# An FFT, a max-of-three layer and a SoLU layer on one core: the weight and first-batch preparation is rebuilt

## The chip, the core and the metric

The kernel runs on one core of a Trainium2 chip. The core has TensorE (PE: matmuls into PSUM; its weight loads are listed apart as PEld), VectorE (DVE), ScalarE (ACT), GpSimd (POOL) and SyncE (SP), whose queue issues every transfer here. Each engine works through its instructions in the order in which they were written. The metric is the device time of one execution in microseconds (us); less is better.

## The reference

```python
def reference(x, moe_w1, moe_w2, moe_w3, moe_w_out, moe2_w_in, moe2_w_out, moe2_g_ln):
    X = np.fft.fft(np.fft.fft(x, axis=1), axis=2).real     # x: 8 x 3072 x 256, f32
    x = X.reshape(8 * 3072, 256)
    h = np.maximum(np.maximum(x @ w1, x @ w2), x @ w3)     # 256 -> 768
    x = h @ w_out                                          # 768 -> 256
    h = x @ w_in                                           # 256 -> 1024
    e = np.exp(h - h.max(-1)); solu = h * e / (e.sum(-1) + 1e-9)
    ln = (solu - mean) / np.sqrt(var + 1e-6) * g_ln
    return ln @ w_out2                                     # 1024 -> 256
```

The weights come as float64, the inputs as float32.

## The kernel before

Each f32 operand is split into two f16 halves (high and low), and a product is three f16 matmuls. The FFT over the sequence is a matmul with a table (`alpha`, over 48 rows), a transposing transfer (`z`) and a second table (`beta`). The FFT over the 256 columns and the sum over real and imaginary parts are folded into the weights ahead of the main work: w1 - w3 and w2 - w3 are multiplied with a cosine and sine table (`wc`), w3 is multiplied with that table (`t3`) and then with w_out (`m3`).

The main work runs over 48 sub-blocks s of 512 rows, six for each of the 8 batches. One sub-block takes two `beta` parts, 14 groups of six `l` matmuls of layer 1 (operations `l1`; two groups for each of six column blocks j, and two with the folded w3), six `m` groups of layer 1's output, four `h` tiles of layer 2's input (12 matmuls each) and four `o` tiles of its output (24 each). Between them ACT, DVE and POOL evacuate (two PSUM buffers hold the `l` groups), take the maximum (`rl`, DVE), split into halves (`rh` on ACT, `rlo` on POOL), and do the exponentials.

Ahead of that stands the **preparation**. `from_f64` turns a weight into f32: a load into a `raw` buffer (`ld`, two buffers), a first pass on ACT (`ga`: magnitude of the high word) and four passes on DVE (`gd`: a maximum, a shift with a mask, and two that merge the high and low words). Then come the subtractions (`sub`, on POOL), `wc`, `t3`, `m3`, the search for each weight's scale (`am`, `dg`, a `spread` matmul, `pow`), and the split into halves. Batch 0 of x goes through `xla` (load), `xgh` (a sum, on DVE), `xfly` (two sums and differences, on POOL), `xsq` (ACT, for the scale), `xsc` (the scale), `xhi`/`xlo` (halves; the low half of chunks 1 and 3 on POOL through `X_POOL`), and `alpha` with its halves `ah` (ACT) and `alo` (DVE).

The order on each engine is written by a planner. `Schedule.run` holds a table of operations with an engine, a planned duration, dependencies, buffers to take and give, and a due value (`vt`, plus an entry of the table `BIAS`); at each step it emits, on the engine that can start first, the operation that ranks first by start and due value. What it emits is a fixed order; on the chip only semaphores delay an instruction. The buffers of the preparation lie in a pool (`prep`) that the second layer's buffers overlay: the operation `open` waits for all operations that were entered with `pop`, and `mh` (the halves for the first `h`) waits for `open`. In this kernel the preparation of w_out2 (operations `f`, `wfg`, `wfm`, `wfs`, `wfn`, `wfh`, `wfl`) is one of them.

Of the kernel before, what the change touches and what calls it, by code (L numbers as in the profile page):

```python
# [1317 lines left out]
```

## Time and profile before

| | us |
|---|---|
| median of 3 runs (2029.46 to 2032.61) | 2031.4 |
| the profiled execution | 2030.42 |
| its span, first to last instruction | 2028.3 |
| PE busy in the span | 1954.3 (96%) |
| DVE / ACT / POOL busy | 1722.3 / 1481.2 / 1343.4 |

About 2 us of the profiled execution lie around the span. Matmuls are pipelined, so that PE's busy time says that it has work in it, not that it is at its peak; PEclk is the TensorE clock that was granted (1.0 is 2.4 GHz, 0.5 is 1.2 GHz).

### The profile page before, as it was taken

To read this page: it belongs to the slowest core of one execution; us is meant where nothing else is said; L and a number is where in the kernel's file an instruction comes from. 1 tells how busy PE (TensorE), PEld (TensorE's weight loads), DVE (VectorE), ACT (ScalarE), POOL (GpSimd) and SP (SyncE) were. 2 spreads that over 40 slices of the span, in tenths; PEclk is the share of its full clock that TensorE was granted. 3 is DMA by queue.
4 is the path that set the end of the run, shared out by engine and by line. 5 is a ranking of instruction groups with operands and counts; after the bars stand their busy time and mean duration, and the time that the engine had idled before them with its cause. 6 is when DMAs were issued, how large, how long until landed. Compare 5 with 4: busy or idle time off the path is not lost.

```text
span 2028.3 us, 40637 instructions
## 1 busy us (share of the span) xinstructions
PE 1954.3 (96%) x14892; PEld 1344.3 (66%) x14892; DVE 1722.3 (85%) x3894; ACT 1481.2 (73%) x2933; POOL 1343.4 (66%) x1408
## 2 busy tenths in 40 slices
PE   3679999999999999999999999999999999999998
PEld 2446666666667666766667666676667666666666
DVE  6878989888898888888888988889888888888884
ACT  3768877877678767786678776787667766766766
POOL 4199986976559756795567856575656565655654
PEclk9789999999999999999999999999999999999999
DMA  7523653543435434444434443333344243333236
GB/s 214 140 64 81 131 115 76 118 95 74 79 69 121 94 69 80 92 113 77 73 72 97 95 84 74 74 63 75 83 74 79 64 84 74 69 74 74 53 69 125
DMA packets 472698, 178.79 MB, mean 88 GB/s; under 512 B 453577, under 2 KB 453802, under 8 KB 469290
## 3 DMA queue, kind: packets, MB, share of 16 engines
q1 hardware_dynamic: 472498, 176.20, 41.7%
q8 instruction: 116, 1.90, 0.4%
q14 instruction: 84, 0.69, 0.1%
HBM read 37.75 MB, written 25.17 MB: 31 GB/s over the span
## 4 chain that ended last, share of the span: by engine, by line
PE 84%; POOL 5%; DVE 5%; ACT 3%; issue 2%; DMA 2%; SPq 0%; POOLq 0%; DVEq 0%; ACTq 0%
PE h L784 22%; PE omm L859 21%; PE l L654 20%; PE m L720 16%; PE beta L549 2%; PE alpha L490 1%; POOL uh L472 1%; POOL xs L410 1%; POOL uv L452 1%; POOL vh L845 1%; POOL rhl L710 1%; DVE v L814 1%; DVE l L675 1%; DMA raw<-in_w_dram 1%; DVE hst L793 1%
## 5 line engine op out<-in xcount | busy, mean ns | idle before, releaser
L710 POOL TENSOR_TENSOR rhl<-sv,rhl 128x512 f16<-128x512 f32 x288 | 333.4, 1160 | 344.2 <-ACT rhl L705 317.5
L859 PE MATMUL omm<-wf,vt 128*128 128x256 f16 x4608 | 533.3, 273 | 1.8 <-ACT ob L866 1.0
L784 PE MATMUL h<-win,mo 128*128 128x512 f16 x2280 | 523.2, 379 | 2.1 <-DVE v L814 2.1
L859 PEld LDWEIGHTS <-vt 128*128 128x128 f16 x4608 | 450.2, 98 | 78.8 <-issue 1.7
L845 POOL TENSOR_TENSOR vh<-v,vh 128x1024 f16<-128x1024 f32 x188 | 400.6, 2131 | 110.8 <-ACT vh L841 107.5
L654 PE MATMUL l<-pq,wl 128*128 128x256 f16 (+2 forms) x3456 | 447.6, 273 | 11.8 <-DVE sv L701 8.1
L675 DVE SCALAR_TENSOR_TENSOR l<-ny,wn,l 128x256 f32<-128x256 f32 (+1 forms) x672 | 318.0, 482 | 148.0 <-ACT bs L367 126.6
L720 PE MATMUL m<-rhl,wo 128*128 128x512 f16 x1728 | 415.2, 380 | 0.0
L654 PEld LDWEIGHTS <-wl 128*128 128x128 f16 x3456 | 332.1, 97 | 111.1 <-issue 10.5
L784 PEld LDWEIGHTS <-mo 128*128 128x128 f16 x2304 | 223.9, 98 | 239.0 <-DVE v L814 3.4
L367 ACT ACTIVATE bs<-l 128x256 f32<-128x256 f32 x560 | 207.4, 380 | 209.2 <-PE l L654 163.9
L819 ACT ACTIVATE jk<-v,hst 128x1024 f16<-128x1024 f32 x192 | 220.1, 1146 | 87.0 <-DVE v L814 86.9
L814 DVE SCALAR_TENSOR_TENSOR v<-h,hst,e 128x1024 f32<-128x1024 f32 x190 | 243.3, 1281 | 29.1 <-ACT e L808 17.0
L720 PEld LDWEIGHTS <-wo 128*128 128x128 f16 x1728 | 163.3, 98 | 151.9 <-issue 1.6
L793 DVE TENSOR_REDUCE hst<-h 128x1 f32<-128x1024 f32 x190 | 231.4, 1218 | 31.6 <-PE h L784 30.3
L808 ACT ACTIVATE e<-h,hst,xb 128x1024 f32<-128x1024 f32 x190 | 228.9, 1205 | 6.4
L841 ACT CAST vh<-v 128x1024 f16<-128x1024 f32 x192 | 200.0, 1042 | 6.0 <-DMA vt<-vh 4.3
L701 DVE SCALAR_TENSOR_TENSOR sv<-l,sv 128x512 f32<-128x512 f32 x288 | 198.2, 688 | 5.7
L705 ACT CAST rhl<-sv 128x512 f16<-128x512 f32 x288 | 176.1, 613 | 35.7 <-DVE sv L701 18.7
L735 POOL TENSOR_TENSOR mo<-s,mw 128x512 f16<-128x512 f32 x96 | 121.6, 1276 | 16.7 <-ACT mw L367 12.2
L832 POOL TENSOR_SCALAR hst<-hst,sc 128x1 f32<-128x1 f32 x192 | 68.1, 354 | 68.7 <-ACT jk L819 56.2
L695 DVE SCALAR_TENSOR_TENSOR sv<-l,bs 128x256 f32<-128x256 f32 x240 | 100.9, 420 | 12.2 <-POOL rhl L710 3.7
(156 smaller groups left out, 2316.2 us busy)
## 6 DMA issues: line engine op xcount, KB each, us to landing
xs<-in_x_dram SPq DMA_DIRECT2D x32, 768.0 KB, 6.3
out_dram<-ob SPq DMA_DIRECT2D x96, 256.0 KB, 2.0
raw<-in_w_dram SPq DMA_DIRECT2D x6, 768.0 KB, 5.0
raw<-in_w_out_dram SPq DMA_DIRECT2D x14, 256.0 KB, 3.4
vt<-vh SPq DMA_TRANSPOSE x192, 4.2
raw<-in_w_in_dram SPq DMA_DIRECT2D x4, 512.0 KB
cb<-in_c_beta_dram SPq DMA_DIRECT2D x1, 1553.0 KB
z<-x SPq DMA_TRANSPOSE x48, 3.3
```

Of the source, the lines that this page charges most:

```text
L367: act.activation(dst, src, AF.Copy, scale=scale)
L654: mm(o, w_[w], hl[:, a, e, c0:c0 + n_], start=(n == 0), stop=(n == 2))
L675: dve.scalar_tensor_tensor(p[:, 0:WA], pq[s][1][:, 0:WA], w, p[:, 0:WA], ALU.mult, ALU.add)
L710: pool.tensor_tensor(t[:, 1], svs.pop((s, j, 0)), t[:, 0], ALU.subtract)
L720: mm(m[:, h], wo[:, w, j, hs], t[:, a], start=(j == 0 and n == 0), stop=(j == NJF - 1 and n == 2))
L784: mm(hp[:, f], m[:, a, d, ts_], win[:, w, d, fs], start=(n == 0), stop=(n == 5))
L793: dve.tensor_reduce(st[:, 0], y["h"], op=ALU.max, axis=AX.XY, negate=True)
L808: act.activation(y["e"], y["h"], AF.Exp, bias=st[:, 11], scale=xbt[s // NSB][:, 12:13], accum_out=st[:, 3])
L814: dve.scalar_tensor_tensor(y["v"], y["h"], st[:, 2], y["e"], ALU.mult, ALU.mult, accum_out=st[:, 4])
L819: act.activation(new(hpool[0], "jk", [128, 2, 512], F16), y["v"], AF.Square, bias=st[:, 4], scale=-float(FF2), accum_out=st[:, 6])
L845: engine.tensor_tensor(y["vh"][:, 1], y["v"].rearrange("p a b -> p (a b)"), y["vh"][:, 0], ALU.subtract)
L859: mm(y["o"][:, 0:D], vt[:, a * 8 + c], wf[:, w, c], start=(n == 0), stop=(n == 23))
```

## The change

The preparation and the start of batch 0 are rewritten:

- **Conversion.** ACT multiplies the high word by 2^-112, which leaves the exponent ready; DVE needs three passes in place of four (the maximum goes, the mask goes with the shift).
- **Buffers.** `raw` has three buffers in place of two, and the two loads of w1 use the memory of `x1`, five in all. w_out2 is loaded into buffers of x (`xs`) and converted into buffers of `uv`, as two pieces of 1024 columns in place of four of 512; its operations, `gl` and `mean` are out of the `prep` pool, so `open` doesn't wait for them. `st` has 8 buffers in place of 9.
- **GpSimd.** `sub` and, for batch 0, `xfly` and all four `xlo` run on DVE. For later batches they stay on POOL.
- **Queue.** `cw` (the cosine table) is loaded first; `cal` (the alpha table) later, and in two pieces of 96 rows and 1. `gl` is loaded in one contiguous piece. Batch 1's loads wait for `open`.
- **Zeros.** Where the planner sees PE idle ahead of an operation, up to the first `h`, `keep_warm` enters matmuls of 512 columns on a tile of zeros (`zz`), for 75% of the planned gap at 216 ns each.
- **The planner's numbers.** Many planned durations are altered and every entry of `BIAS` (some 250) is replaced, so that all orders change.

```diff
-EXP_MIN = float(np.array(0x38000000, np.int32).view(np.float32))
+EXP_SHIFT = 2.0**-112
...
-                vh=2, vt=3, ob=2, xb=4, dg=1, raw=2, st=9)
-X_POOL = (0, 1, 0, 1)
+                vh=2, vt=3, ob=2, xb=4, dg=1, raw=3, st=8)
...
-BIAS = {("xla", 0): -477.352, ("xgh", 0): 585.07, ("xfly", 0): 58.101, ("xsq", 0): 186.462, ("xhi", 0): 986.332,
...
+BIAS = {("xla", 0): -534.137, ("xgh", 0): 286.232, ("xfly", 0): -6.751, ("xsq", 0): 385.004, ("xhi", 0): 285.602,
...
-PORT = {"gd", "wlo", "w3l", "vl", "xgh", "xlo"}
+PORT = {"gd", "sub", "wlo", "w3l", "vl", "xgh", "xfly", "xlo"}
...
+            if o.eng == "PE" and self.idle:
+                self.idle(k, start - clock["PE"])
...
+    def x_buffer():
+        return new(fp, "xs", [128, GC * 2 * D], F32)
...
+    def uv_buffer():
+        return new(fp, "uv", [128, 4 * D], F32)
...
-        t = new(fp, "xs", [97, GC, 2, D], F32)
+        t = x_buffer()[0:97].rearrange("p (g w d) -> p g w d", g=GC, w=2)
...
-    def x_fly(b, c):
+    def x_fly(b, c, engine):
...
-        u = new(fp, "uv", [97, 2, GC, 128], F32)[0:n]
+        u = uv_buffer()[0:n].rearrange("p (h g d) -> p h g d", h=2, g=GC)
         for h, o in enumerate((ALU.add, ALU.subtract)):
-            pool.tensor_tensor(u[:, h], t[:, :, 0:128], t[:, :, 128:256], o)
+            engine.tensor_tensor(u[:, h], t[:, :, 0:128], t[:, :, 128:256], o)
...
-        op(("xla", *k), "SP", 3500, x_load, k, v - 0.5, deps=[("xla", b, c - 1)] if c else [("xla", b - 1, NCH - 1)] * (b > 0) + [("gd", "f", 3)] * (b == 1),
...
-        op(("xfly", *k), "Pool", 2450, x_fly, k, v - 0.2, deps=[("xgh", *k)], take=["uv"], give=["xs"])
+        op(("xla", *k), "SP", 3500 if b else 2600, x_load, k, v - 0.5, deps=[("xla", b, c - 1)] if c else [("xla", b - 1, NCH - 1)] * (b > 0) + [("open",), ("gd", "f", 1)] * (b == 1),
...
+        op(("xfly", *k), *(("Pool", 2450) if b else ("DVE", 1200)), x_fly, (*k, pool if b else dve), v - 0.2, deps=[("xgh", *k)], take=["uv"], give=["xs"])
...
-        normed = 1 if b else X_POOL[c]
+        normed = b > 0
...
-                op(("al", *kh), "PE", 520, alpha_mm, kh, v + 0.04 * h, deps=[("xlo", b, c)] + [("al", b, 0, 0)] * (not first) + [("al", b, c, 0)] * h,
+                op(("al", *kh), "PE", 520, alpha_mm, kh, v + 0.04 * h, deps=[("xlo", b, c), ("cal",)] + [("al", b, 0, 0)] * (not first) + [("al", b, c, 0)] * h,
...
-        sp.dma_start(cal, c_alpha)
+        sp.dma_start(cal[0:96], c_alpha[0:96])
+        sp.dma_start(cal[96:97], c_alpha[96:97])
...
-    ones = tp.tile([128, 128], F32, name="ones")
+    zz = wp.tile([128, 512], F16, name="zz")
+    pool.memset(zz, 0.0)
+    ones = wp.tile([128, 128], F32, name="ones")
...
-    const_load()
+    op(("cal",), "SP", 900, const_load, (), -0.85, lag=2000)
...
+    def f64_home(key, home):
+        if home == "raw":
+            return new(tp, "raw", [128, FF, 2], I32)
+        if home == "xs":
+            return x_buffer().bitcast(I32).rearrange("p (m w) -> p m w", w=2)
+        if home not in homes:
+            homes[home] = new(fp, "x1", [128, NSB, 2, 4, 128], F16).rearrange("p s h q x -> p (s h q x)").bitcast(I32)
+        return homes[home][:, key[-1] * 2 * FF:(key[-1] + 1) * 2 * FF].rearrange("p (m w) -> p m w", w=2)
...
-        def magnitude():
-            act.activation(dst(), raws[key].bitcast(F32)[:, 0:n, 1], AF.Abs)
-
-        slow, fast = 80 + 1.145 * n, 110 + 0.585 * n
-        return magnitude, [
-            (fast, lambda: dve.tensor_scalar(dst(), dst(), EXP_MIN, None, ALU.max)),
-            (fast, lambda: dve.tensor_scalar(bits(), bits(), 3, 0x3FFFFFFF, ALU.logical_shift_left, ALU.bitwise_and)),
-            (slow, lambda: dve.scalar_tensor_tensor(bits(), word(1), -0x40000000, bits(), ALU.bitwise_and,
+        def exponents():
+            act.activation(dst(), raws[key].bitcast(F32)[:, 0:n, 1], AF.Copy, scale=EXP_SHIFT)
+
+        slow, fast = 15 + 1.135 * n, 30 + 0.6 * n
+        return exponents, [
+            (fast, lambda: dve.tensor_scalar(bits(), bits(), 3, None, ALU.logical_shift_left)),
+            (slow, lambda: dve.scalar_tensor_tensor(bits(), word(1), -0x80000000, bits(), ALU.bitwise_and,
                                                     ALU.bitwise_or)),
             (slow, lambda: dve.scalar_tensor_tensor(bits(), word(0), 29, bits(), ALU.logical_shift_right,
                                                     ALU.bitwise_or)),
         ]
...
-        pop(("ld", *key), "SP", 4.4 * n, f64_load, (key, srcs, n), v - 0.2, deps=after, take=["raw", *take], lag=2000)
...
+        put(("ld", *key), "SP", 3.4 * n, f64_load, (key, srcs, n, home), v - 0.2, deps=after, take=[home] * first + [*take], lag=1900)
...
-        pool.tensor_tensor(wrs[i, a], wrs[i, a], wrs[0, a], ALU.subtract)
+        dve.tensor_tensor(wrs[i, a], wrs[i, a], wrs[0, a], ALU.subtract)
...
-            from_f64((i, a), [w[a * 128:(a + 1) * 128]], w_first(i, a), FF, -0.9 + 0.1 * i + 0.03 * a, take=["st"])
+            from_f64((i, a), [w[a * 128:(a + 1) * 128]], w_first(i, a), FF, -0.9 + 0.1 * i + 0.03 * a, take=["st"],
+                 **(dict(home="x1", first=a == 0, after=[("ld", 1, 0)] * a, done=[("gd", 1, 0)] * a, give=[("x1", ("ld", 1, 0))] * a) if i == 1 else {}))
...
-            pop(("sub", i, a), "Pool", 1760, w_sub, (i, a), v, deps=[("gd", i, a), ("gd", 0, a)])
+            pop(("sub", i, a), "DVE", 890, w_sub, (i, a), v, deps=[("gd", i, a), ("gd", 0, a)])
...
-            pop(("wc", i, a), "PE", 4000, w_dft, (i, a), v, take=["mh"[a]],
+            pop(("wc", i, a), "PE", 2600, w_dft, (i, a), v, take=["mh"[a]],
...
-        pop(("m3", e), "PE", 5100, w3_mm, (e,), -0.5,
+        pop(("m3", e), "PE", 2620, w3_mm, (e,), -0.5,
...
-    gl = tp.tile([128, 8], F32, name="gl")
-    pop(("gl",), "SP", 600, lambda: sp.dma_start(gl, g_ln.rearrange("(c p) -> p c", p=128), allow_slow_non_contiguous=True), (), 0.0,
-        lag=2500)
+    gl = wp.tile([128, 8], F32, name="gl")
+    op(("gl",), "SP", 400, lambda: sp.dma_start(gl, g_ln), (), 0.0, lag=2000)
...
-        for c in (2 * u, 2 * u + 1):
+        for c in range(4 * u, 4 * u + 4):
...
-    for u in range(4):
...
+    for u in range(2):
...
-        from_f64(("f", u), [w_out2[c * 128:(c + 1) * 128] for c in (2 * u, 2 * u + 1)], staged(w2r, u // 2, slice(u % 2 * 512, (u % 2 + 1) * 512)),
-                 512, v, take=[] if u % 2 else ["st"], after=[("ld", "f", u - 1)] if u else staged_first)
-        pop(("wfg", u), "ACT", 800, wf_gain, (u,), v, deps=[("gd", "f", u), ("gl",)])
-    pop(("wfm",), "PE", 5300, wf_mean, (), 0.5, deps=[("wfg", u) for u in range(4)], take=["misc"])
-    pop(("wfe",), "ACT", 270, wf_mean_ev, (), 0.5, deps=[("wfm",)], give=["misc"])
+        from_f64(("f", u), [w_out2[c * 128:(c + 1) * 128] for c in range(4 * u, 4 * u + 4)], w2_staged(u), 1024, v, take=["uv"], home="xs",
+                 after=[("ld", "f", u - 1)] if u else [("xla", 0, NCH - 1)], put=op)
+        op(("wfg", u), "ACT", 1620, wf_gain, (u,), v, deps=[("gd", "f", u), ("gl",)])
+    op(("wfm",), "PE", 3450, wf_mean, (), 0.5, deps=[("wfg", u) for u in range(2)], take=["misc"])
+    op(("wfe",), "ACT", 270, wf_mean_ev, (), 0.5, deps=[("wfm",)], give=["misc"])
     for u in range(2):
...
-    prep_keys.append(("wfc",))
...
+    spare = {}
+
+    def keep_warm(key, gap):
+        if key[0] == "h":
+            sch.idle = None
+            return
+        tag = "h" if ("l1", 0, 0, 0) in spare else "l1"
+        spare[key] = True
+        n = int(gap * 0.75 / 216)
+        if n and tag not in spare:
+            spare[tag] = new(ps, tag, [128, 2, 512] if tag == "h" else [128, 512], F32, "spare")
+        for _ in range(n):
+            p = spare[tag]
+            mm(p[:, 0] if tag == "h" else p, zz[:, 0:128], zz)
+
+    sch.idle = keep_warm
```

The SP queue at the start, before (a row is line, transfer, destination and source; `x2` is two in a row):

```order
L905 DMA cal<-in_c_alpha_dram 97x577
L931 DMA raw<-in_w_dram 128x1536 x2
L403 DMA xs<-in_x_dram 96x2048
L405 DMA xs<-in_x_last_dram 1x2048
L931 DMA raw<-in_w_dram 128x1536 x2
L403 DMA xs<-in_x_dram 96x2048
L1203 DMA gl<-in_g_ln_dram 128x8x1
L908 DMA cw<-in_c_w_dram 128x514
```

and in the change, where `x_115` is the memory of `x1`:

```order
L915 DMA cw<-in_c_w_dram 128x514
L951 DMA raw<-in_w_dram 128x1536 x2
L409 DMA xs<-in_x_dram 96x2048
L411 DMA xs<-in_x_last_dram 1x2048
L951 DMA x_115<-in_w_dram 128x1536
L409 DMA xs<-in_x_dram 96x2048
L951 DMA x_115<-in_w_dram 128x1536
L409 DMA xs<-in_x_dram 96x2048
L1225 DMA gl<-in_g_ln_dram 128x8
```

`cal`, the only large transfer of 97 rows, has left the front, and nothing that waits for a buffer stands ahead of the seventh large load.

DVE after the first two conversions, before (L947 to L951 are the four passes, L410 is `xgh`):

```order
L410 TENSOR_TENSOR xs<-xs 97x4x256
L947 TENSOR_SCALAR st<-st 128x768
L948 TENSOR_SCALAR st<-st 128x768
L949 SCALAR_TENSOR_TENSOR st<-raw,st 128x768
L951 SCALAR_TENSOR_TENSOR st<-raw,st 128x768
L947 TENSOR_SCALAR st<-st 128x768
L948 TENSOR_SCALAR st<-st 128x768
L410 TENSOR_TENSOR xs<-xs 96x4x256
```

and in the change (L967 to L970 the three passes, L416 `xgh`, L458 `xfly`, L990 `sub`):

```order
L416 TENSOR_TENSOR xs<-xs 97x4x256
L458 TENSOR_TENSOR uv<-xs 97x512 x2
L967 TENSOR_SCALAR st<-st 128x768
L968 SCALAR_TENSOR_TENSOR st<-x_115,st 128x768
L970 SCALAR_TENSOR_TENSOR st<-x_115,st 128x768
L416 TENSOR_TENSOR xs<-xs 96x4x256
L990 TENSOR_TENSOR st<-st 128x768
L458 TENSOR_TENSOR uv<-xs 96x512 x2
```

`xfly` and `sub` now stand in DVE's own queue, and one pass in four is gone.

PE from its first work on, before (L1067 is `t3`, L976 `wc`, L983 a one-column product of the folded weights, L423 the sum for x's scale, L490 `alpha`):

```order
L1067 MATMUL prep<-cw,st 128x256 x12
L976 MATMUL prep<-st,cw 128x384 x8
L983 MATMUL prep<-cw,st 128x1 x6
L423 MATMUL total<-xb,unit 128x4
L976 MATMUL prep<-st,cw 128x384 x4
L490 LDWEIGHTS uh
```

and in the change the stretch around the first `wc` (L1315 is a matmul on zeros):

```order
L1315 LDWEIGHTS zz
L1315 MATMUL spare<-zz 128x512
L996 MATMUL prep<-st,cw 128x384 x8
L1315 LDWEIGHTS zz
L1315 MATMUL spare<-zz 128x512
L1315 LDWEIGHTS zz
L1315 MATMUL spare<-zz 128x512
L429 MATMUL total<-xb,unit 128x4
L1315 LDWEIGHTS zz
L1315 MATMUL spare<-zz 128x512
```

Matmuls on zeros now stand between the operations; there are 149 of them, 39 ahead of the first `t3`, and all ahead of the first `h`.

## Rows read from the trace of the kernel before

**Rows 1.** The page's 40 slices of the span: PE busy and granted clock, tenths.

```profile
PE   3679999999999999999999999999999999999998
...
PEclk9789999999999999999999999999999999999999
```

**Rows 2.** Stretches: length, busy us and count per engine, PEclk, DMA share, GB/s.

```profile
2.50:5.00 2.50, 0.00 (x0) 0.00 (x0) 0.00 (x0) 0.00 (x0) 0.00 (x0) 1.00 0.97 323
...
10.00:12.50 2.50, 0.00 (x0) 0.00 (x0) 0.00 (x0) 0.28 (x1) 0.00 (x0) 1.00 0.10 27
...
12.20:55.00 42.80, 21.90 (x62) 15.35 (x63) 36.83 (x37) 19.77 (x32) 22.52 (x14) 0.88 0.69 212
55.00:90.00 35.00, 22.05 (x156) 17.01 (x154) 28.68 (x57) 22.97 (x49) 6.48 (x4) 0.74 0.38 104
...
93.00:147.35 54.35, 39.15 (x244) 25.37 (x242) 40.08 (x100) 39.49 (x80) 44.30 (x30) 0.82 0.33 82
147.35:200.00 52.65, 49.11 (x410) 32.88 (x408) 46.34 (x115) 46.23 (x89) 48.90 (x46) 1.00 0.41 91
200.00:1900.00 1700.00, 1697.47 (x13104) 1167.38 (x13103) 1477.01 (x3389) 1263.04 (x2520) 1152.02 (x1225) 1.00 0.42 84
```

**Rows 3.** PE's timeline: start, length, line, shape, count, idle before.

```profile
36.52 5.32 PE L976 MATMUL prep<-st,cw 128*128 128x384 f32 x16
...
49.90 5.28 PE L976 MATMUL prep<-st,cw 128*128 128x384 f32 x8
...
55.64 1.11 PE L490 MATMUL alpha<-cal,uh 97*128 97x96 f16 x22 [0.37 <-DVE uh L370]
...
66.98 5.29 PE L1079 MATMUL prep<-st 128*128 128x256 f32 x12
...
90.02 1.46 PE L549 MATMUL beta<-cb,z 128*128 128x64 f16 x24 [4.29 <-DMA z<-x]
...
92.99 2.75 PE L654 MATMUL l<-pq,wl 128*128 128x256 f16 x12
...
147.35 2.75 PE L784 MATMUL h<-win,mo 128*128 128x512 f16 x12
```

**Rows 4.** ACT's timeline, the first pass over the first weight.

```profile
12.22 0.89 ACT L943 ACTIVATE st<-raw 128x768 f32<-128x768 f32 x1 [10.22 <-DMA raw<-in_w_dram]
```

**Rows 5.** The page's list of transfers: count, size, median us to landing.

```profile
raw<-in_w_dram SPq DMA_DIRECT2D x6, 768.0 KB, 5.0
```

**Rows 6.** DVE's timeline.

```profile
13.14 0.56 DVE L947 TENSOR_SCALAR st<-st 128x768 f32<-128x768 f32 x1 [13.14 <-ACT st L943]
13.74 0.56 DVE L948 TENSOR_SCALAR st<-st 128x768 int32<-128x768 int32 x1
14.33 0.96 DVE L949 SCALAR_TENSOR_TENSOR st<-raw,st 128x768 int32<-128x768 int32 x1
15.33 0.96 DVE L951 SCALAR_TENSOR_TENSOR st<-raw,st 128x768 int32<-128x768 int32 x1
...
26.41 2.04 DVE L948 TENSOR_SCALAR st<-st 128x768 int32<-128x768 int32 x1
28.37 1.21 DVE L410 TENSOR_TENSOR xs<-xs 96x1024 f32<-96x1024 f32 x1
...
54.30 1.28 DVE L370 SCALAR_TENSOR_TENSOR uh<-uv,xb,uh 97x1024 f16<-97x1024 f32 x1 [1.25 <-ACT uh L367]
...
84.02 1.01 DVE L525 TENSOR_TENSOR x<-alpha,x 128x384 f16<-128x384 f32 x2
...
142.60 0.68 DVE L724 SCALAR_TENSOR_TENSOR s<-m,s 128x512 f32<-128x512 f32 x1
```

**Rows 7.** DVE's groups from 93 to 147.35 us: busy, mean ns, idle before.

```profile
L675 DVE SCALAR_TENSOR_TENSOR l<-ny,wn,l 128x256 f32<-128x256 f32 x21 | 10.0, 484 | 11.2 <-ACT bs L367 11.0
L701 DVE SCALAR_TENSOR_TENSOR sv<-l,sv 128x512 f32<-128x512 f32 x9 | 6.1, 683 | 0.1
L695 DVE SCALAR_TENSOR_TENSOR sv<-l,bs 128x256 f32<-128x256 f32 x10 | 4.2, 417 | 0.2
```

More of the change, by code (lines that the diff above doesn't have):

```diff
@@ L103, in _holds_port @@
         return False
-    if isinstance(key[0], str) and key[0] == "os3":
-        return key[-1] != 0
     return key[0] in PORT
@@ L237, in __init__ @@
     def __init__(self, capacity):
-        self.ops = {}
+        self.ops, self.idle = {}, None
         self.free = {tag: [0.0] * n for tag, n in capacity.items()}
@@ L764, in fft_moe_solu_kernel @@
                give=["m", "pq"] if h else [])
-            op(("mh", *k), "ACT", 1050, mo_hi, k, v, deps=[("ma", *k), ("open",)] + [("mh", s, 0)] * h,
+            op(("mh", *k), "ACT", 1185, mo_hi, k, v, deps=[("ma", *k), ("open",)] + [("mh", s, 0)] * h,
                take=["mw"] if h else ["mo", "mw"])
@@ L953, in f64_parts, with from_f64 @@
         ]
-    def from_f64(key, srcs, dst, n, v, take=(), after=()):
-        pop(("ld", *key), "SP", 4.4 * n, f64_load, (key, srcs, n), v - 0.2, deps=after, take=["raw", *take], lag=2000)
-        magnitude, parts = f64_parts(key, dst, n)
-        pop(("ga", *key), "ACT", 95 + 0.83 * n, magnitude, (), v, deps=[("ld", *key), *after])
-        prep_keys.append(("gd", *key))
-        sch.chain(("gd", *key), "DVE", parts, (), v, deps=[("ga", *key)], give=["raw"])
+    def from_f64(key, srcs, dst, n, v, take=(), after=(), home="raw", first=True, give=None, done=(), put=pop):
+        put(("ld", *key), "SP", 3.4 * n, f64_load, (key, srcs, n, home), v - 0.2, deps=after, take=[home] * first + [*take], lag=1900)
+        exponents, parts = f64_parts(key, dst, n)
+        put(("ga", *key), "ACT", 95 + 0.95 * n, exponents, (), v, deps=[("ld", *key), *after])
+        if put is pop:
+            prep_keys.append(("gd", *key))
+        sch.chain(("gd", *key), "DVE", parts, (), v, deps=[("ga", *key), *done], give=[home] if give is None else give)
     def staged(table, key, cols):
@@ L995, in bound, with pow2_scale @@
         act.activation(unused, t(), AF.Abs, accum_out=am[:, col:col + 1])
-    def pow2_scale(key, c0, n, deps, v):
+    def pow2_scale(key, c0, n, deps, v, put=pop):
         t = am[:, c0 + n:c0 + 2 * n]
-        pop((key, "dg"), "ACT", 200 * n, lambda: diagonal(key, am[:, c0:c0 + n]), (), v, deps=deps, take=["dg"])
-        pop((key, "all"), "PE", 250 * n, lambda: spread(key), (), v, deps=[(key, "dg"), ("eye",)], take=["misc"], give=["dg"])
+        put((key, "dg"), "ACT", 305 * n, lambda: diagonal(key, am[:, c0:c0 + n]), (), v, deps=deps, take=["dg"])
+        put((key, "all"), "PE", 250 + 100 * n, lambda: spread(key), (), v, deps=[(key, "dg"), ("eye",)], take=["misc"], give=["dg"])
         sch.chain((key, "pow"), "DVE", [(150 + 130 * n, lambda: over_partitions(key, t)), (72, lambda: at_least(t, t)),
                                         (72, lambda: pow2(t))], (), v, deps=[(key, "all")], give=["misc"])
-        prep_keys.append((key, "pow"))
+        if put is pop:
+            prep_keys.append((key, "pow"))
     def recip(col, c):
@@ L1218, in wf_mean @@
         tmp["mean"] = p
-    mean = tp.tile([128, D], F32, name="mean")
+    mean = wp.tile([128, D], F32, name="mean")
     def wf_mean_ev():
```

109 lines of the change are left out of this document (57 added, 52 removed), and 55 rows, old and new, of the table BIAS.

## The prediction

> **What bounds the kernel now.** I looked first at PE's busy slices against its clock, then at a table of stretches, then at the timelines of the early ones. The slices show a kernel of two parts: from about the fifth of 40 on PE is full at full clock, ahead of that it isn't, and there the clock is often low [rows 1]. The table says it sharply: from 200 to 1900 us PE is busy 1697.47 of 1700 us, DVE 87%, POOL 68% [rows 2]. No edit can win there except by taking PE work away, and this one takes none away. So the end is set by how early the first `h` comes, from where PE is nearly full: 147.35 us [rows 3]. What follows it takes 2030.4 - 147.35 = 1883.1 us, with the 2 us outside the span. I make the sum against this execution; the median of the runs is 1 us above it.
>
> The first 147 us have three stretches. To 55 us (the first `alpha`) DVE is busy 36.83 of the 42.8 us since its first operand landed, so DVE is the limit [rows 2]. But part of that is not work: the same 768-column shift takes 0.56 us with POOL idle and 2.04 us while POOL works on `xfly` [rows 6]. From 55 to 90 us (first `beta`) it is a chain over PE, ACT and DVE, with PE at 0.74 of its clock. From 93 us (first `l`) to 147.35 us no engine is full: POOL 44.30, DVE 40.08, ACT 39.49 of 54.35 us [rows 2]; PE waits for DVE, DVE for ACT's evacuations (11.2 us ahead of L675 [rows 7]), and POOL spends part of its time on batch 1's x and w_out2.
>
> **The start.** The first weight lands at 12.2 us [rows 4], though loads of that size take 5.0 us from issue to landing in the median [rows 5]. From 10 us on the core moves only 27 GB/s [rows 2]: something narrow finishes last, and the first conversion waits for it. The queue holds `cal` with 97 rows there; the change takes it out. With the median of 5.0, an issue at about 1.5 us and 0.8 us for `cw` ahead of it I take 7.5 us; if the tail isn't `cal`, it stays at 12.2. The Trainium skill, "DMA: Bandwidth & Descriptors", section "Why a DMA increments its semaphore by 16 and not by 1", says that a transfer is spread over the largest number of DMA engines up to 16 that divides its row count, and gives 127 partitions as a case of one engine. 97 is prime too; by this rule and the page's 27 GiB/s per engine, `cal`'s 109 KB would take some 3.8 us alone (an estimate), and the first weight would land about that much earlier, at 8.4. The trickle in the trace agrees with it, but does not prove whose it is.
>
> **DVE to the first `alpha`.** ACT's pass takes 0.9 us [rows 4], so DVE starts at 8.4. Then, by the clean rows [rows 6]: six conversions of 0.56 + 0.96 + 0.96 = 2.48 us, 14.9 (the fourth pass, 0.56 each, is gone); four `xgh` of 1.21, 4.8; eight halves of `xfly`, whose price on DVE the trace doesn't show: half of `xgh`'s columns, 0.61 each, 4.9 (between 0.5 by a clean pass and 1.2 as a whole `xgh`); four `sub` of 768 columns, 0.91 each by the same row, 3.6; the first half of w_out2, 1024 columns, 3.3; five short ones for x's scale, 0.8. Sum 32.3, so the first low half starts at 40.7 and is done at 42.0 (1.28 us). POOL has nothing to stretch them with. What was POOL's becomes 8.5 us of DVE, still less than what four passes and the stretching cost: before, this point is at 54.3 + 1.3. Beside it, the second `wc` ends at about 42.2: its 16 passes take 5.3 us at full clock, as the first `wc`'s did, where before eight of them took 5.28 at half clock [rows 3]. I say `alpha` at 43, against 55.6: 12.6 earlier. Loads must keep up: the queue moves about 9.2 MB up to the first half of w_out2, 28 us at the 323 GB/s of the first transfers [rows 2], so it lands near 31 to 33, ahead of its place in DVE's queue at 37. DMA isn't on the path, with some 4 us to spare.
>
> **`alpha` to `beta`.** DVE has eight `alo` (two take 1.01 [rows 6]: 4.0), two conversions of w_out, 5.0, the other half of w_out2, 3.3, three low halves, 3.8, four low halves of the layer-1 weights, 768 columns at the 0.96 of such a pass, 3.8, the maximum over the folded w3, 0.7, and short ones, 2.0: 22.6. `m3` (12 passes took 5.29 at half clock [rows 3], so 5.3 for both at full) stands between the second conversion of w_out and that maximum, and I add 2 us of waiting. So the last `alo` ends at 43.7 + 22.6 + 2 = 68.3, against 85.0. Before, 5.0 us later comes `beta` and 3.0 after that the first `l` [rows 3, 6]: now 73.3 and 76.3.
>
> **First `l` to first `h`.** Up to the second sum of layer 1 (`ma`), DVE's order in the change holds 17 L675-type products at 0.484, 8.2; 17 pairs at about 0.84, 14.3; six maxima at 0.683, 4.1 [rows 7]; two `ma` at 0.68, 1.4; the halves of `beta` and of w3, 2.0; what is left of w_in's conversions, 4.3; 15 short ones, 2.6. That is 36.9 us, starting 0.9 before the first `l`. From that `ma`'s end (143.3 [rows 6]) to the first `h` it took 4.1, so 40 us in all, against 54.4. Back-to-back instructions overlap by some 0.07 us each, over 75 of them 5 us, which leaves room for that much waiting. ACT's list in the same stretch, counted in the same way, is about as long (33 us); POOL's falls from 44 to some 24, since batch 1's x and w_out2's subtractions are out of it. `open` no longer waits for w_out2, but in before `mh` waits for `ma` anyway, so this earns nothing by itself. Bounds: 36 with no waiting, 53 if DVE waits as often as before (74% busy). I take 40, so `h` at 116.3.
>
> **The rest.** At the first `h` the change has done 21 groups of `l` and 7 of `m`, before 22 and 8; the two come later, 0.7 us (a quarter of the first twelve at half clock) and 1.3 (half an `h`) [rows 3]. Sum: 1883.1 + 2.0 + 116.3 = 2001.4, say **2001 us**, 29 less. The last `h` and `o` stand in the same order as before. The 149 matmuls on zeros cost 0.216 us each by the `h` row, 32 us, all inside planned gaps; 39 stand ahead of the first `t3`, 8.4 us at full and 17 at half clock, and `t3` has until the first `sub` of w1, near 27, so they hide. Where a gap turns out shorter than planned they delay: at most 7 us for the 32 after the first `l`.
>
> **The rivals.**
> *The clock stays low* (10%). Before, with PE idle a third of the time, it was granted 0.74 and 0.82 on average [rows 2]. If zeros in three quarters of the planned gaps aren't enough, since real gaps are longer, the second `wc`, `m3` and the mean of w_out2 cost 5 + 5 + 3 more on the path: 2014.
> *The ramp keeps its length* (25%). ACT's queue now holds w_out2's and w_in's passes between the evacuations, and the two PSUM buffers of `l` tie PE, ACT and DVE into one round. If DVE stays at 74%, the ramp takes 53 instead of 40: 2014. For it speaks that before no engine was full there; against it, that POOL was the fullest and loses 20 us.
> *All goes without waiting* (8%): `alpha` at 42, `beta` at 71, 36 to `h`: 1993.
> *The new order costs in the steady part* (4%, the slower side). Every `BIAS` entry changes, and batch 1's 19 us of POOL work move behind the first `h`. Were each of the 47 sub-blocks after it to lose 0.62 us of PE, for instance because an `rlo` (POOL) queues behind a longer one and `m` waits, the 29 us would be gone; at 0.8 it would be 2001 + 38 = 2039. Against it: POOL is a third idle there and PE now waits 2.5 us in 1700.
> *Nothing comes of it* (2%), the early gains being given back in the ramp.
> The forecast itself has about 51%, between 1994 and 2008.
>
> **How the numbers follow.** The range 1990 to 2016 takes in the forecast, the clean case, the low clock and most of the ramp case, with the late first load (+4.7) inside it: about 85%. A measurement here tells 0.2% (4 us) from no change; by the cases above faster 0.94, within it 0.02, slower 0.04.
>
> **What would show it.** First conversion on ACT near 7.5; DVE's shifts all near 0.5 us; PEclk near 1.0 from 25 to 125 us; `alpha` near 43, last `alo` near 68, first `l` near 76, first `h` near 116; from 200 us on PE full as before. Wrong would be: ACT's first pass still at 12; `m3` at 5.3 us per six matmuls; over 45 us from `l` to `h`; or PE idle over 5 us between 200 and 1900.

## The result, and the profile after

The changed kernel takes 2001.35 us in the median of four runs. One of them, at a mean clock of 0.752, took 2560.15 and stays out of the comparisons below; the other three took 1998.01, 1999.85 and 2002.85, with 1999.85 as their median. The kernel before takes 2031.04 beside it: ratio 0.9848, 95% interval 0.9831 to 0.9864. Run again with the experiments, it took 1998.95 (ratio 0.9843, 0.9829 to 0.9856). The forecast was 2001, with a range of 1990 to 2016. The profiled execution took 2002.85.

First the page's slices, for [rows 1]: PE's busy share and the granted clock. PE's busy time holds the zeros, so that a 9 says less than it did; the clock row, in slices of 50 us, has lost its dips.

```profile
PE   8899999999999999999999999999999999999998
...
PEclk9999999999999999999999999999999999999999
```

The table of stretches, for [rows 2] (length, busy us and count for each engine, PEclk, DMA share, GB/s), here cut at the milestones of the change:

```profile
7.50:43.00 35.50, 30.91 (x120) 18.09 (x119) 32.39 (x43) 18.79 (x33) 0.73 (x1) 0.90 1.02 319
43.00:73.00 30.00, 27.16 (x202) 19.05 (x201) 22.96 (x41) 23.80 (x46) 6.80 (x4) 0.95 0.22 66
...
76.00:118.00 42.00, 37.22 (x277) 21.95 (x278) 36.74 (x96) 33.40 (x70) 21.90 (x17) 0.96 0.33 73
...
170.00:1900.00 1730.00, 1727.81 (x13408) 1189.93 (x13407) 1487.73 (x3451) 1308.87 (x2577) 1185.78 (x1252) 1.00 0.42 84
```

In the first stretch DVE is busy 32.39 of 35.50 us, and the DMA engines are at 1.02 of their time: both are full or nearly so. Between 76 and 118 us, about the stretch from the first `l` to the first `h`, POOL has 21.90 us of work, where before it had 44.30 in that stretch. Behind it PE is full, as before.

PE's timeline, for [rows 3]: first `wc`, sum of x's squares, second `wc`, `alpha`, `m3`, `beta`, `l`, `h`.

```profile
26.79 4.78 PE L996 MATMUL prep<-st,cw 128*128 128x384 f32 x14 [1.93 <-DVE st L990]
...
34.13 0.36 PE L429 MATMUL total<-xb,unit 128*128 128x4 f32 x2 [2.13 <-ACT zj L425]
...
38.02 7.64 PE L996 MATMUL prep<-st,cw 128*128 128x384 f32 x16
45.49 1.19 PE L496 MATMUL alpha<-cal,uh 97*128 97x96 f16 x24
...
53.25 5.70 PE L1101 MATMUL prep<-st 128*128 128x256 f32 x24 [0.38 <-ACT wn L1010]
...
76.11 0.88 PE L555 MATMUL beta<-cb,z 128*128 128x64 f16 x24 [0.86 <-DMA z<-x]
...
78.11 1.76 PE L660 MATMUL l<-pq,wl 128*128 128x256 f16 x12
...
118.37 2.89 PE L790 MATMUL h<-win,mo 128*128 128x512 f16 x12
```

The first `h` has come forward by 29.0 us and the end of the span by 27.2; 1.8 are given back behind `h`. The second `wc` took 7.64 us: the clock had dropped (0.50 from 36 to 42 us) after PE had been idle for 2.13 us. ACT's first pass, for [rows 4]:

```profile
5.72 0.90 ACT L963 ACTIVATE st<-raw 128x768 f32<-128x768 f32 x1 [3.71 <-DMA raw<-in_w_dram]
```

DVE's timeline, for [rows 6]:

```profile
29.45 1.22 DVE L416 TENSOR_TENSOR xs<-xs 96x1024 f32<-96x1024 f32 x1 [1.25 <-DMA xs<-in_x_dram]
...
40.16 2.47 DVE L370 SCALAR_TENSOR_TENSOR uh<-uv,xb,uh 97x1024 f16<-97x1024 f32 x2
46.72 0.56 DVE L531 TENSOR_TENSOR x<-alpha,x 128x384 f16<-128x384 f32 x1 [4.09 <-ACT x L527]
...
69.55 1.07 DVE L531 TENSOR_TENSOR x<-alpha,x 128x384 f16<-128x384 f32 x2 [0.81 <-ACT x L527]
```

Before the first row DVE waits 1.25 us for a load of x (with 0.54 and 0.50 earlier for other loads, 2.3 in all), and before the third it waits 4.09 us for the late `alpha`.

### The profile page after: what moved, and what is told of

It is laid out like the page before. It is cut to its first block, busy times and chain, and to the rows that moved or that the text cites. A ratio compares the mean times of both kernels' runs of the same rounds, so it can differ in the third digit from the quotient of the medians.

```text
span 2001.1 us, 40923 instructions
## 1 busy us (share of the span) xinstructions
PE 1975.3 (99%) x15041; PEld 1348.0 (67%) x15041; DVE 1696.1 (85%) x3886; ACT 1493.0 (75%) x2929; POOL 1315.2 (66%) x1395
## 4 chain that ended last, share of the span: by engine, by line
PE 82%; DVE 6%; POOL 5%; ACT 3%; DMA 3%; issue 2%; SPq 0%; POOLq 0%; DVEq 0%; ACTq 0%
PE omm L865 22%; PE h L790 21%; PE l L660 19%; PE m L726 16%; PE beta L555 2%; PE alpha L496 1%; POOL uv L458 1%; DMA xs<-in_x_dram 1%; DVE l L681 1%; POOL xs L416 1%; POOL vh L851 1%; POOL rhl L716 1%; DMA vt<-vh 1%; ACT jk L825 1%; POOL mo L741 1%
## 5 line engine op out<-in xcount | busy, mean ns | idle before, releaser
L799 DVE TENSOR_REDUCE hst<-h 128x1 f32<-128x1024 f32 x190 | 231.7, 1219 | 50.7 <-PE h L790 49.7
L872 ACT ACTIVATE ob<-omm,hst 128x256 f32<-128x256 f32 x192 | 89.9, 469 | 57.6 <-PE omm L865 42.1
```

The lines of the kernel that those rows point to most:

```text
L799: dve.tensor_reduce(st[:, 0], y["h"], op=ALU.max, axis=AX.XY, negate=True)
```

## The experiments

Milestones, in us, all from the timelines of PE, ACT and DVE; "low" is the start of the first low half of x, the last column the median of the runs, for the changed kernel without the run of 2560.15:

| kernel | ACT's first pass | low | alpha | last alo ends | first l | first h | span | time |
|---|---|---|---|---|---|---|---|---|
| changed | 5.72 | 40.16 | 45.49 | 70.62 | 78.11 | 118.37 | 2001.1 | 1999.85 |
| changed_again | 5.58 | 38.79 | 40.78 | 66.53 | 73.55 | 112.58 | 1995.4 | 1998.95 |
| no_zeros | 5.83 | 40.11 | 42.26 | 69.73 | 76.54 | 116.54 | 2001.3 | 2004.55 |
| cal_ahead_split | 6.49 | 40.66 | 42.66 | 68.13 | 75.60 | 115.05 | 1998.3 | 1999.42 |
| cal_ahead_97 | 13.28 | 46.29 | 48.28 | 73.42 | 81.04 | 120.42 | 2003.5 | 2004.67 |
| pool_share | 5.83 | 44.88 | 46.55 | 71.75 | 79.68 | 118.54 | 2002.5 | 2004.28 |
| four_passes | 5.56 | 42.02 | 43.90 | 71.47 | 78.69 | 118.84 | 2001.6 | 2003.83 |
| four_undone | 13.01 | 56.76 | 58.74 | 87.38 | 94.11 | 134.67 | 2024.4 | 2026.22 |

**The baseline: changed_again.** No edit.

> The changed kernel as it is, once more, for the baseline of the single edits and for the second wc: in seven executions of its relatives these 16 passes took 5.3 to 5.4 us or 7.0 to 8.2. Theory: the half clock falls now on the end of the first wc, now on the second, from one execution to the next. So the second wc takes 5.3 us here (then alpha near 42, first h near 115) or 7 to 7.7 (then 45 and 118), and the median lies at 1998 to 2003. Rival: the 7.64 us belong to this order of instructions, and come again as they were.

```profile
35.62 5.32 PE L996 MATMUL prep<-st,cw 128*128 128x384 f32 x16
40.78 1.19 PE L496 MATMUL alpha<-cal,uh 97*128 97x96 f16 x24
...
112.58 2.90 PE L790 MATMUL h<-win,mo 128*128 128x512 f16 x12
```

The theory holds: the same kernel, 5.32 us at full clock this time, and the first `h` 5.8 us earlier. The order does not fix the half clock, and two executions of this kernel can differ by some 6 us. Part of that began before the second `wc`: PE had been idle for 0.95 us ahead of the sum of x's squares, not for 2.13, where the load of x that had held DVE up at 29 us came in time. Single edits are therefore compared by medians, with 1999.0, the median over seven runs of the changed kernel, as base. The intervals of the ratios are some 3 us wide to either side, and those of the edits overlap a little with that of this run. Of the 28 pairs of a run with a single edit (no_zeros, cal_ahead_97, pool_share, four_passes) and one without, 24 to 26 are slower with it; by means in place of medians these edits cost 4.4, 4.6, 4.3 and 4.0 us. So each of them very likely costs something; which of them costs most is open.

**The zeros: no_zeros and before_zeros.**

```diff
-    sch.idle = keep_warm
```

> The changed kernel without its 149 matmuls on zeros; everything else stands in the same order. Theory: the zeros hold the clock, and the early passes of PE stand on the path. Then the granted clock between 7.5 and 43 us falls below 0.8 (0.90 with zeros), the 16 passes of the second wc and the 12 of m3 take near 10 us each instead of 7.6 and 5.7, and the first h comes 5 to 12 us later than 118.4: 2007 to 2014 us. Rival: PE waits for DVE and the loads at the head of these passes anyway, so slower passes fill idle time. Then the clock falls as well, but the first h stays within 2 us of 118.4 and the time is 2000 to 2004.

Stretches, first of the changed kernel, then without the zeros (the last two lines):

```profile
25.00:43.00 18.00, 14.04 (x44) 8.55 (x45) 16.27 (x24) 11.95 (x20) 0.73 (x1) 0.81 1.02 358
```

```profile
25.00:43.00 18.00, 14.59 (x62) 9.24 (x63) 17.14 (x25) 12.64 (x22) 0.73 (x1) 0.81 1.02 352
43.00:76.00 33.00, 21.81 (x174) 18.77 (x172) 26.32 (x49) 24.35 (x49) 7.02 (x4) 0.75 0.32 89
```

The clock did not fall where the theory had it: from 7.5 to 43 us it is 0.90 with the zeros and 0.90 without (0.81 and 0.81 behind 25 us; changed_again has 1.00). It fell to 0.75 between 43 and 76 us, where it was 0.95, and the time rose by 5.5 us to 2004.55 (ratio to before 0.9864, 0.9849 to 0.9878), below the theory's range and just above the rival's. The prices were wrong too: the second `wc` took 5.41 us without any zeros, and `m3` 6.52 instead of near 10. From 34 to 44 us the clock was at 1.00 without them; only the last 14 passes of the first `wc` (7.13 us instead of 4.78) lost much. `h` was 1.8 us earlier than in the first profiled execution, as the rival allowed, and 4.0 later than in the second. Behind `h` this execution took 1886.5 us, where the first took 1884.5; 1.4 of that is a longer wait of PE for ACT ahead of its last 72 passes. So the time is slower, but the trace does not show the theory's path.

> The kernel before with the changed kernel's rule for matmuls on zeros added (0.75 of each gap that the planner sees on PE ahead of the first h; 198 of them), its orders unchanged. Theory: the half clock between 49 and 125 us stood on the path of before only in part, since PE had idle time to catch up in. Then the granted clock there rises from 0.64 to 0.77 to over 0.9, and the time falls by 2 to 8 us: 2023 to 2030. Rival: the clock is the greater part of the gain: 2005 to 2020. It could also be slower, where a planned gap is in truth shorter and the zeros delay the PE work behind them: 2033 to 2038.

The time did not fall: 2032.85 against 2031.8 (ratio 1.0008, 0.9999 to 1.0018), just below the third range. Stretches, first of the kernel before, then with the zeros (the last two lines):

```profile
76.00:100.00 24.00, 14.07 (x110) 10.96 (x111) 18.86 (x50) 15.46 (x37) 1.94 (x2) 0.64 0.77 186
100.00:118.00 18.00, 13.23 (x64) 9.23 (x63) 11.63 (x29) 13.38 (x28) 14.97 (x10) 0.74 0.29 75
```

```profile
76.00:100.00 24.00, 20.49 (x156) 12.86 (x156) 20.58 (x57) 17.10 (x40) 3.50 (x3) 0.93 0.84 200
100.00:118.00 18.00, 14.76 (x84) 9.29 (x82) 11.00 (x26) 13.08 (x27) 15.21 (x11) 1.00 0.22 56
```

The clock is 0.93 and 1.00 there, where without zeros it was 0.64 and 0.74 (from 49 to 76 us it is 0.84, where it was 0.75), and little came of it: `h` started at 146.27 instead of 147.35. But the run does not price the clock alone, since the zeros stood in the way of the second `wc`. PE's timeline with them:

```profile
50.30 4.00 PE L1292 MATMUL spare<-zz 128*128 128x512 f16 x9
54.10 2.83 PE L980 MATMUL prep<-st,cw 128*128 128x384 f32 x8
```

Nine zeros at half clock took 4.00 us there, so that these eight passes, twice as fast as before, started at 54.10 instead of 49.90, and `alpha` at 56.77 instead of 55.64. From there to `h` it took 89.5 us instead of 91.7. So the better clock gave some 2 us back behind `alpha`, and the zeros took 1 of them ahead of it; from `h` to the end this execution took 1886.5 us instead of 1883.1, some 2 of it in longer waits of PE in the last 20 us. That most of before's slow passes lay in time in which PE would have waited is likely, not shown.

**The load of `cal`: cal_ahead_split, cal_ahead_97, before_cal_split.** `cal` is issued ahead of everything (the last three lines), as two transfers or, with the first three lines, as one; the third kernel is that of before with the split alone.

```diff
-        sp.dma_start(cal[0:96], c_alpha[0:96])
-        sp.dma_start(cal[96:97], c_alpha[96:97])
+        sp.dma_start(cal, c_alpha)
...
-    op(("cal",), "SP", 900, const_load, (), -0.85, lag=2000)
+    const_load()
+    op(("cal",), "SP", 900, lambda: None, (), -0.85, lag=2000)
```

> The changed kernel with cal (its 96 rows and its one row as two transfers) issued ahead of all other loads. Both theories expect the same here: the first pass of ACT moves from 5.7 us by the 111 KB ahead of it, at most 0.6 us, and the time stays at 2000 to 2003. It is the control of the run with 97 rows in one transfer. A first pass near 10 would say that being ahead in the queue is what costs, not the 97 rows.

> The changed kernel with cal as one transfer of 97 rows, issued ahead of all other loads as in the kernel before. Theory: one transfer of 97 rows is what the first weight waited for. Then ACT's first pass comes at 10 to 12.2 us instead of 5.7, the loads behind it are late by as much, and the first h is 3 to 6 us later: 2004 to 2008. Rival: the 12.2 us of before had another cause (cw far behind in the queue, or the two first weights in another order). Then the first pass is where it is with cal in two transfers, within 0.3 us, and so is the time.

> The kernel before with one thing changed: cal is sent as 96 rows and one row, at its old place ahead of all. Theory: DVE sets the pace from its first operand on there too, so that most of the 6 us by which the first weight lands earlier (12.2 to near 6) comes through: the first alpha at 49 to 52 instead of 55.6, the first h 3 to 6 us earlier than 147.35, 2025 to 2028. Rival: PE's first t3 waits for cw, POOL for x, both far behind in the queue, and the gain is lost there or in the 54 us before the first h: 2029 to 2033.

ACT's first pass, in one fence for each kernel (ahead in two transfers, ahead with 97 rows, before with the split):

```profile
6.49 0.91 ACT L964 ACTIVATE st<-raw 128x768 f32<-128x768 f32 x1 [4.48 <-DMA raw<-in_w_dram]
```

```profile
13.28 0.89 ACT L963 ACTIVATE st<-raw 128x768 f32<-128x768 f32 x1 [11.27 <-DMA raw<-in_w_dram]
```

```profile
6.05 0.89 ACT L944 ACTIVATE st<-raw 128x768 f32<-128x768 f32 x1 [4.05 <-DMA raw<-in_w_dram]
```

The same bytes at the same place: 6.8 us later with 97 rows in one transfer (13.28, above the theory's 10 to 12.2; the split ahead moved the pass by 0.8 us, forecast at most 0.6). That `cal`'s 97 rows in one transfer are what the first weight waited for is now shown, and not only argued. The tail itself, in the kernel before:

```profile
12.50:15.00 2.50, 0.00 (x0) 0.00 (x0) 1.79 (x3) 1.51 (x2) 0.00 (x0) 1.00 0.06 26
```

A share of 0.06 is about that of one DMA engine of 16. The Trainium skill, "DMA: Bandwidth & Descriptors", section "Why a DMA increments its semaphore by 16 and not by 1", spreads a transfer over the largest number of engines up to 16 that divides its row count, which for 97 rows is one; that share and the delay agree. The delay is larger than the prediction's estimate of 3.8 us, and why is open. Of the 6.8 us, 5.3 reach the end (2004.67 against 1999.42 with the split). In the kernel before, two lines of code bring 6.6 us by themselves (2025.44 against 2032.07; ratio 0.9970, 0.9958 to 0.9981). `alpha` comes at 49.50 (its first two passes at 48.19), where it was 55.64 (55.02), and `h` at 142.45, 4.9 earlier, as the theory had it; the two profiled executions differ by 4.7. This part needs none of the others.

**DVE and POOL: pool_share.** Work goes back to POOL at the same places of the order.

```diff
-        op(("xfly", *k), *(("Pool", 2450) if b else ("DVE", 1200)), x_fly, (*k, pool if b else dve), v - 0.2, deps=[("xgh", *k)], take=["uv"], give=["xs"])
+        op(("xfly", *k), *(("Pool", 2450) if b else ("DVE", 1200)), x_fly, (*k, pool), v - 0.2, deps=[("xgh", *k)], take=["uv"], give=["xs"])
...
-        dve.tensor_tensor(wrs[i, a], wrs[i, a], wrs[0, a], ALU.subtract)
+        pool.tensor_tensor(wrs[i, a], wrs[i, a], wrs[0, a], ALU.subtract)
```

> The changed kernel with batch 0's xfly and the subtractions of w1 and w2 given back to POOL at the same places of the order; DVE's list is 8.9 us shorter for it. Theory: DVE and POOL hold each other up, so that DVE's 768-column shift takes over 1 us where POOL works (0.56 alone), the low halves of x end 3 to 8 us later than 42.6, and the first h with them: 2003 to 2009. Rival: what an engine has to do is all that counts. Then DVE has its low halves done by 38 to 42 us, bound by the loads, the second wc starts no later than 38, and the time is 1998 to 2002.

DVE's timeline, then POOL's:

```profile
26.45 2.83 DVE L967 TENSOR_SCALAR st<-st 128x768 int32<-128x768 int32 x1
29.31 2.44 DVE L968 SCALAR_TENSOR_TENSOR st<-raw,st 128x768 int32<-128x768 int32 x1
```

```profile
25.73 3.13 POOL L458 TENSOR_TENSOR uv<-xs 96x512 f32<-96x512 f32 x2 [2.03 <-DVE xs L416]
28.82 2.12 POOL L990 TENSOR_TENSOR st<-st 128x768 f32<-128x768 f32 x1
```

The theory holds: 5.3 us slower than 1999.0, though DVE has 8.9 us less to do. Its shift of 768 columns, 0.55 us alone, takes 2.83 and ends 0.4 us behind POOL's two instructions, and the next pass, 0.96 alone, takes 2.44 and ends 0.8 us behind POOL's `sub`; the mean of the six shifts is 1.58 us. POOL's `sub` is stretched too: the first of the four took 2.67 us, the last 1.80, and the first `wc` waits 4.63 us for the second of them. So an instruction can be held up here without waiting for a semaphore: it then shows as busy for longer. The Trainium skill, "SBUF — State Buffer", section "SBUF: two separate sides", describes a port pair that whichever of the two engines starts first holds for its whole instruction; these rows agree.

**Three passes or four: four_passes.**

```diff
+        def shifts():
+            dve.tensor_scalar(bits(), bits(), 1, None, ALU.logical_shift_left)
+            dve.tensor_scalar(bits(), bits(), 2, None, ALU.logical_shift_left)
...
-            (fast, lambda: dve.tensor_scalar(bits(), bits(), 3, None, ALU.logical_shift_left)),
+            (fast, shifts),
```

> The changed kernel with the shift by three bits made as two passes of DVE, by one and by two bits, in all 14 conversions, so that each has four passes on DVE again: six more passes of 0.56 us ahead of the first alpha (and one of 0.68), the others up to the first h. Theory: DVE sets the pace from its first operand to the last alo, except for the 2.3 us in which it waits for loads. Then the low halves of x end 1.5 to 4 us later than 42.6, the last alo 3 to 6.5 us later than 70.6 (or than 68, where the second wc has full clock), the first h 3 to 8 us later than 115 to 118, and the time is 2002 to 2009. Rival: the loads set the pace from 10 us on, and the fourth pass fills DVE's waits. Then nothing moves by more than 1.5 us: 1998 to 2002.

It cost 4.8 us (2003.83, in the theory's range). The low halves start at 42.02, 1.9 to 3.2 later than in the two executions without, for 4.0 us of passes ahead of them; DVE's 1.0 to 2.3 us of waiting for loads are gone. So both were partly right: the loads hide a part.

**The stretch before the first `h`: pool_filler.**

```diff
         pool.tensor_tensor(t[:, 1], svs.pop((s, j, 0)), t[:, 0], ALU.subtract)
+        for _ in range(7 if sch.idle else 0):
+            pool.tensor_tensor(load, load, load, ALU.subtract)
...
+    load = wp.tile([128, 128], F32, name="load")
+    pool.memset(load, 0.0)
```

> The changed kernel with work on POOL that nothing waits for: behind each of the first eight rlo, up to the first h, seven subtractions of 128x128, some 20 us together, about what w_out2's subtractions and batch 1's x took of POOL in the kernel before (112 to 150 us). Theory: the stretch from the first l to the first h became shorter because that work left POOL. Then it grows from 40 us to 46 to 54, and the time to 2005 to 2014. Rival: the order of the other engines made it shorter (halves of w3 and of w_in earlier, products of DVE packed), and POOL has room: it stays within 2 us of 40, and the time at 1998 to 2004.

The time was 2014.9 (ratio 0.9917, 0.9902 to 0.9931), 0.9 above the theory's range. POOL's group of the fillers from 76 to 123.6 us (busy, mean ns of one, idle before), and PE's timeline:

```profile
L718 POOL TENSOR_TENSOR load<-load 128x128 f32<-128x128 f32 x48 | 20.1, 419 | 3.2
```

```profile
101.25 1.24 PE L728 MATMUL m<-rhl,wo 128*128 128x512 f16 x4 [2.43 <-POOL rhl L716]
...
114.60 1.02 PE L728 MATMUL m<-rhl,wo 128*128 128x512 f16 x4 [2.10 <-POOL rhl L716]
...
123.56 0.59 PE L792 MATMUL h<-win,mo 128*128 128x512 f16 x2
```

From the first `l` (73.84) to the first `h` it now takes 49.7 us instead of 39 to 40, and PE waits for POOL's `rlo` ahead of `m`: 9.2 us in all, where in changed_again it waited for none. That POOL's fillers only held DVE up, as in pool_share, is ruled out by DVE's rows, whose larger groups all keep their length but for the conversions (three passes at 0.90 us in the mean for 0.68). The other 6 of the 16 us are lost behind `h`. So a load of that size on POOL would have undone 10 of the 14 us won in this stretch. That it is what was won in the real kernel is made likely, not shown: the fillers stand directly behind each `rlo`, w_out2's and batch 1's work stood elsewhere.

**The table: old_table.** The entries of BIAS are those of before; all else is the change.

> The changed kernel with the numbers of BIAS from the kernel before, so that every order is the planner's own with those numbers; all else of the change stays. Theory: the parts of the change, not the table, carry the gain. Then first alpha is at 43 to 48, first h at 116 to 125, the rest as long as before within 3 us: 2000 to 2010. Rival: the gain comes from the table, which places the work of the first 120 us and of the 47 sub-blocks behind it. Then the first h is later than 130, or the stretch behind it longer by over 5 us, and the time over 2015.

The first `h` came at 121.63, as the theory had it, but the time was 2081.08, as the rival had it (ratio 1.0237, 1.0222 to 1.0253): from 400 to 1900 us PE was busy 1475.38 of 1500, with the full kernel's 1498.56 beside it; that is 23 of the some 76 us by which the stretch behind `h` is longer. I do not conclude that the table carries the gain: the old numbers belong to another graph with other durations, so this prices a table used in the wrong place, and is inconclusive on new against old. But it shows how much hangs on it: the rival that a new order costs in the steady part was no idle thought.

**Four parts together: four_undone.** The edits of no_zeros, cal_ahead_97, pool_share and four_passes in one kernel.

> The changed kernel with four parts undone together: no zeros, cal as one transfer of 97 rows ahead, xfly and the subtractions on POOL, the shift in two passes; the orders, the places of the buffers and w_out2 outside the overlay stay. Undone singly they cost 3 to 5 us (no_zeros), 3 to 5 (cal_ahead_97), 3 to 5 (pool_share) and 2.5 to 4.5 (four_passes) over 1999.4 to 2001.4. Theory: they lie behind each other on one path, so they add up: 12 to 19 over the changed kernel, 2012 to 2020, with the first h at 127 to 136; what is then left to 2031 belongs to the order and to what left POOL before the first h. Rival: each takes time that another has already left idle (the later load fills DVE's waits, the fourth pass too): 2005 to 2010.

It took 2026.22 (ratio to before 0.9969, 0.9956 to 0.9981), above the theory's range. The theory's rule held, its base did not: over 1999.0 the single edits cost 5.5, 5.7, 5.3 and 4.8, 21.3 in all, and together 27.2 (by means 17.2 and 25.5). In the table `alpha` moves by 1.5, 7.5, 5.8 and 3.1 against changed_again, 17.9 in all, and by 18.0 together: they lie behind each other. PE's rows show the new wait:

```profile
40.29 7.74 PE L1000 MATMUL prep<-st,cw 128*128 128x384 f32 x14 [9.32 <-POOL st L994]
...
94.11 0.40 PE L660 MATMUL l<-pq,wl 128*128 128x256 f16 x1
...
134.67 1.24 PE L790 MATMUL h<-win,mo 128*128 128x512 f16 x5
```

From `l` to `h` it is still 40.6 us, against 54.4 before: that part of the gain needs none of the four. Yet only 5.9 us are left to 2032.07, since `alpha` (58.74) comes 3.1 later than before (55.64), and the stretch behind the first `h` took 1889.7 us instead of 1882.8. Of these 6.9, some 4 lie in the last 20 us (PE waits 3.23 us for ACT there, where it waited 1.72 in the changed kernel, and its last 72 passes, those of the last `o` tiles (`omm`), take 10.79 us instead of 8.16); for the others I have no cause.

**More zeros: more_zeros.** Twelve more ahead of the sum of x's squares, of w1's mean column and of the second `wc`.

```diff
+EXTRA = {("xall", 0): 8, ("wcn", 1): 2, ("wc", 2, 0): 2}
...
+        n += EXTRA.get(key, 0)
```

> The changed kernel with 12 more matmuls on zeros: eight ahead of the sum over x's squares, where PE stood idle for 2.13 us, two ahead of the mean column of w1 and two ahead of the second wc. Theory: the half clock under the second wc followed from that idle time; with it filled the pass takes 5.3 us in each execution, alpha starts at 41 to 43, the first h at 114 to 116, and the time is 1996 to 2000. Rival: 2.6 us of zeros stand in the way of the sum and of the second wc, and the first h comes no earlier than without them: 2000 to 2004.

The second `wc` took 5.32 us, `h` came at 114.91, and the five runs lie between 1998.19 and 2000.81 (median 1999.33), the profile and the median as the theory had them; the seven runs of the changed kernel lie between 1997.18 and 2004.95. But the median is no lower than that of changed_again, so the run does not tell a mended dip from a lucky execution.

## Why the prediction was right

**What bounds it** held: PE is busy 1727.81 of 1730 us, and the end is the first `h` plus a constant. Behind `h` the profiled execution took 1884.5 (2002.85 - 118.37); the sum said 1883.1 + 2.0 = 1885.1. The clean case of the rivals (1993) leaves the 2.0 out; with it, 71 + 3 + 36 + 1885.1 makes 1995. The seven runs lie from 1997 to 2005, so that a median within 2 us of the forecast is in part luck.

**The start** was early: the first pass at 5.72, not 7.5. The cause was the right one; the size was the median of [rows 5], 5.0 us, of which issue (1.5) and `cw` (0.8) leave 3.4 here.

**DVE to the first `alpha`** came out at 40.16 for 40.7, but as two errors that cancel. DVE started 1.8 us early (6.65 for 8.4) and lost 2.3 us to loads. "DMA isn't on the path, with some 4 us to spare" is the step that failed: from 7.5 to 43 us the DMA engines were at 1.02, and three loads came only after DVE was ready for them. I had counted the bytes up to one point, and not load by load against DVE's list. The rows' prices held (0.64 for half an `xfly`, forecast 0.61; `sub` 0.95, forecast 0.91). One reading was wrong: the shift of 2.04 us in [rows 6] (26.41 to 28.45) stands beside POOL's `sub`, not beside `xfly`. POOL's timeline of before:

```profile
25.91 2.13 POOL L970 TENSOR_TENSOR st<-st 128x768 f32<-128x768 f32 x1 [2.09 <-DVE st L951]
```

The conclusion holds, since both have left POOL.

**The second `wc` at full clock** failed in the profiled execution (7.64 for 5.3, hence `alpha` at 45.49 for 43) and held in changed_again (5.32; 40.78). The zeros do not hold the clock in every execution: from 25 to 125 us PEclk was 0.93, where near 1.0 was forecast.

**From `alpha` to `beta` and `l`**: the last `alo` ended 2.3 us after the forecast, `l` came 1.8 after, all of it carried over from `alpha`, which came 2.5 after. **From `l` to `h`**: 40.3, forecast 40.

**The rivals.** The low clock was priced at 13 us; without any zeros the kernel loses 5.5. I had charged every half-clock pass to the path; the second `wc` and most of `m3` had full clock without zeros. The ramp that keeps its length did not come, and pool_filler shows what it takes to bring it back. Of the other three, changed_again came near the case without waiting up to `beta` (`alpha` at 40.78, `beta` at 71.55) but not behind it (39.0 us from `l` to `h`, not 36); the other two stayed away.

**Where the 33 us went** (2032 to 1999): the transfer of 97 rows 5.7, POOL away from DVE 5.3, a pass of DVE saved 4.8, the zeros 5.5, each uncertain by some 3, and 6 more when all four go at once, for which part of the cause is open. The rest of 6 is what order, buffers, batch 1 and w_out2 keep of their 14 us between `l` and `h`; how it divides among them no run tells.

## What to carry to other kernels

Where the end is a constant behind one event, cost every edit by what it does to that event, and price stage by stage. Look at the row counts of the transfers at the head of a queue before anything larger: two lines were worth 6.6 us of 33. A low clock costs only where the slow pass, and not a wait beside it, sets the next step, and matmuls on zeros cost where the pass behind them is waited for; before_zeros had a better clock and no better time, and both may have had a part in it. And a table of order numbers can cost more with another graph (80 us in old_table) than the whole change wins.

## What the runs showed of the hardware

The half clock moves within one kernel. In the first profiled execution it fell on the second `wc`, in changed_again on neither, and in cal_ahead_split, which differs by one early load, on the first (0.50 from 30 to 32 us, 14 passes in 6.47 us instead of 4.78). The length of the idle time ahead does not settle it: with 1.93, 1.93 and 2.20 us ahead of them (changed, changed_again, four_passes) these 14 passes took 4.78 us, with 1.95 and 2.00 (cal_ahead_split, pool_filler) 6.47. Stretches of the first, with PE's idle 2 us ahead:

```profile
32.00:34.00 2.00, 0.00 (x1) 0.00 (x0) 2.00 (x5) 1.19 (x4) 0.00 (x0) 1.00 1.13 376
...
36.00:38.00 2.00, 2.00 (x10) 1.93 (x10) 1.97 (x7) 1.42 (x5) 0.00 (x0) 0.50 0.94 361
38.00:40.00 2.00, 2.00 (x5) 1.07 (x4) 1.97 (x2) 2.00 (x4) 0.73 (x1) 0.50 1.05 387
```

PE stands idle at the first row; at the others it is fully at work, at the lower of its two levels (0.50, 1.2 GHz).
